# Attention and expert layer on one core: the first block's down projection, the weights' maxima and the output queue are rearranged

## The chip, the cores and the metric

The kernel runs on one core of a Trainium2 chip. The metric is the device time of one execution in microseconds (us). The inputs are float32 and lie in the chip's memory.

## The reference

The program has two parts. The first is attention: for each of 4 batches, `kv` (384 x 32 positions of 128 channels) is averaged over 4 x 4 positions, multiplied by `w_sr`, and used as keys and values of 12288 queries. The second is a layer of 8 experts over all 49152 rows x of the attention's output. Cut to what matters:

```python
a = softmax(scale * q @ k.T); x = a @ v
do = x @ w_skip > 0                      # other rows are passed on as they are
e = argmax(x[do] @ w_gate); g = softmax(x[do] @ w_gate)[e]
y = g * (relu(x @ w1[e]) @ w2[e])        # w1[e]: 128 x 1024, w2[e]: 1024 x 128
out[do] = x + y
```

## The kernel before

The attention phase takes the rows in 384 tiles of 128. When a tile group is done, its rows are written to the output and routed: the rows of each expert are scattered to a region of a scratch tensor `scr` in device memory, by GpSimd's indirect DMAs (line 192), one for 128 rows. Each row carries its gate, its row number in the output and a scale.

The expert layer then works on groups of 2048 rows of one expert, each in 4 blocks of 512 rows (`NST = 4`). Six groups of the expert that has most rows are peeled out of the loop and follow the attention in one straight program (`peel`, line 419, 24 blocks); the other groups run in a loop (line 1105) whose number of rounds is known only at run time. Here it is 12. All matrix operands are split in two float16 halves, high and low, and a product is a sum of three: high x high, high x low and low x high. In the peel and in the loop each engine runs its instructions in the order in which the program emits them.

A block s works as follows.

- `finish` (line 323) empties the accumulators of the block before: VectorE computes gate x y + x from the accumulator's first 128 columns (line 342), ScalarE takes the second 128 columns (line 330), GpSimd adds both (line 335) and scatters the rows to the output (line 192), in 4 tiles of 128 rows. The row numbers are read from column C + 1 of the block's x tile `xin`. In the peel, VectorE copies them first (line 354), since there the rows are put in a queue, `out_rows`, and scattered later.
- `up` (line 291) computes 8 chunks of h = relu(x @ w1): three products of 512 columns each (lines 296 to 298) into one of 4 PSUM buffers, from which ScalarE takes the high half (line 299) and VectorE the low half (line 300).
- `gates` (line 319) makes the block's factors on VectorE.
- `x_transpose` (line 280) splits the x of the block after next (ScalarE line 282, VectorE line 285) and transposes it by a DMA on SP's queue (line 289).
- `load_x` (line 197) loads the x of a coming block into the buffer that the block before has left.
- `down` (line 303) adds h @ w2 into 4 accumulators: for each of 8 chunks k, four products of high h with the 256 columns of w2's high and low halves, which lie side by side in `w2_hl`, and, one chunk later, four products of low h with the 128 columns of the high half (line 309).

The weights of the next group come in over the four blocks. In block 0, `split_w2` (line 274) splits this group's w2: ScalarE writes the high half (line 275), VectorE the low half (line 276), and a copy of the output scale follows (line 278). Then the next w1 and w2 are loaded (lines 257, 260). In block 1, `w_scale` (line 200) takes the largest magnitude of each (line 209) and writes them on two diagonals (line 217). In block 2 one product spreads them over the partitions (line 220) and the scales follow. In block 3, `split_w1` (line 230) splits w1.

The rows in the peel are sent by `scatter_next` (line 363), which is called five times per block, at its top, after up chunks 0, 1 and 3 and inside the down projection, and a sixth time after chunk 5 if no row for `scr` is left. It sends a row tile to `scr` if one is left and at most 20 output row tiles (`(HOLD - 1) * TT`) are queued, and an output row tile otherwise. `finish` queues two of a block's four tiles at the block's top and two after chunk 3. The buffers of the output rows are 6 (`HOLD`), taken in turn, so a block's `finish` must wait until the rows of the sixth block before are written. The loads of the loop's first weights are emitted in the step in which no row for `scr` is left (`flush`, line 920), on SP's queue.

The loop is divided into stages, one block each, and an engine enters a stage only when all have left the stage before last; `previous_stage_wait` (line 1113) puts that wait at a place of its own on an engine. On SP in block 0, the loads of the weights stand behind the first four up chunks, and the load of x stands ahead of the transpose.

Of the kernel before, what the change touches and what calls it, by code (L numbers as in the profile page):

```python
# [25 lines left out]
def kernel(  # L26
# [142 lines left out]
    h, paced, scr_rows, out_rows, first_p, held = {}, {}, [], [], [], []  # L169
# [30 lines left out]
    def w_scale(halves=False):  # L200
        em = emask.broadcast_to([P, 2])
        for i, w in enumerate((w1_raw, w2_raw.rearrange("p k c -> p (k c)"))):
# [5 lines left out]
            else:  # L208
                nc.vector.tensor_reduce(out=w_max[:, i:i + 1], in_=w, axis=AX.X, op=ALU.max, apply_absolute_value=True)
        if halves:  # L210
            nc.vector.tensor_reduce(out=w_max, in_=w_part, axis=AX.X, op=ALU.max)
# [4 lines left out]
        for i in range(2):  # L216
            eng.tensor_scalar(out=w_dg[:, i, :], in0=ident_bf, scalar1=wf[:, i:i + 1], scalar2=None, op0=ALU.mult)
# [30 lines left out]

    def load_w(gidx):
        load_expert(nc.sync.value_load(tabi[0:1, bass.ds(gidx, 1)], min_val=0, max_val=E - 1))  # L250

    def load_expert(e):
        load_w1(e)
        load_w2(e)
# [48 lines left out]
    def down(s):  # L303
        terms = []
        for c in range(FC + DL):
            terms.extend((x, k, n) for x, k, n in (("hi", c, 2), ("lo", c - DL, 1)) if 0 <= k < FC)
        for i, (x, k, n) in enumerate(terms):
            for t in range(TT):
                m = nc.tensor.matmul(ys[t][:, 0:n * C], h[x][:, k, t * P:(t + 1) * P],  # L309
                                     w2_hl[:, k, 0:n, :].rearrange("p a c -> p (a c)"), start=(i == 0),  # L310
# [12 lines left out]
    def finish(s, end=False):  # L323
        o = (first_p[0] if first_p else op).tile([P, TT, C], F32, name="o")
        o2 = None if end else op.tile([P, TT, C], F32, name="o2", bufs=1)
        ids = xin[s].bitcast(I32)
# [5 lines left out]
        def send(ts):  # L332
            for t in ts:
                if not end:
                    nc.gpsimd.tensor_tensor(out=o[:, t, :], in0=o[:, t, :], in1=o2[:, t, :], op=ALU.add)  # L335
                if first_p:
                    out_rows.append((out, kept[:, t:t + 1], o[:, t, :], NT - 1, "out"))
                else:
                    scatter_rows(out, ids[:, t, C + 1:C + 2], o[:, t, :], NT - 1, "out")

        for t in range(TT):
# [10 lines left out]
        if first_p:  # L352
            kept = first_p[0].tile([P, TT], I32, name="ids")
            nc.vector.tensor_copy(kept, ids[:, :, C + 1])
        else:
            yield
# [6 lines left out]
    def scatter_next():  # L363
        if held:
            return
        if scr_rows and len(out_rows) <= (HOLD - 1) * TT:
# [52 lines left out]
    def peel():  # L419
        LB = PEEL * NST  # L420
        for b in range(LB):
# [9 lines left out]
            for c in range(FC):  # L431
# [4 lines left out]
                if b == LB - 3 and c == 5:  # L436
                    scale = w_scale()
                if b in (LB - 3, LB - 2) and c == 5:
                    next(scale, None)
# [734 lines left out]
```

## Time and profile before

| | |
|---|---|
| median of 3 runs | 1758.96 us (1758.93 to 1760.55) |
| the profiled execution, its own time | 1756.8 us |
| its span, first to last instruction | 1754.2 us |
| TensorE busy | 1700.2 us, 97% of the span |
| VectorE, ScalarE, GpSimd busy | 87%, 75%, 66% |
| mean granted clock of TensorE | 0.997 |

The rows below and all numbers of the prediction come from the profiled execution. Times of a timeline count from the start of its span. The timeline merges neighbours of one kind: a line gives the start of the first, the time until the end of the last, and their number. Products overlap: a product of 512 columns is shown with 0.38 us, but starts 0.22 us after the one before it. So TensorE's pace is read from the starts, and its idle time in brackets, which counts from a product's shown end, is shorter than the time lost. PE is TensorE, DVE VectorE, ACT ScalarE, POOL GpSimd, SP the queue of most loads and of the transposes. The attention phase ends at about 970 us, the peel at about 1219, the loop at about 1744.

### The profile page before, as it was taken

The numbers are of one execution on the slowest core, as the hardware profiler recorded it, in microseconds if no ns is written. First come the engines' busy times: TensorE is split into PE (matmuls) and PEld (weight loads), VectorE is DVE, ScalarE is ACT, GpSimd is POOL, SyncE is SP. The second block draws the span as 40 slices with busy tenths as digits, with TensorE's granted clock in tenths as the row PEclk, the third lists the DMA queues.
The fourth block names the chain that finished last, engine by engine and source line by source line (L and its number), as shares of the span: only waits on it lengthen the run. The fifth ranks groups of instructions, "written<-read, shape, count | busy, mean of one in ns | idle before, by whom it ended". The sixth has DMA issues, their size and how long they took to land. (4 is left out here: it accounts for less than half of the span.)

```text
span 1754.2 us, 47456 instructions
## 1 busy us (share of the span) xinstructions
PE 1700.2 (97%) x16497; PEld 1393.2 (79%) x16497; DVE 1532.2 (87%) x3221; ACT 1311.9 (75%) x2683; POOL 1156.6 (66%) x1576
## 2 busy tenths in 40 slices
PE   6999999999999999999999999999999999999997
PEld 5999999999999989999998666676666666666665
DVE  7989999999999999999999867777888888888886
ACT  4888888888888888888888656666666666666664
POOL 3368778888788887666566667755555555555554
PEclk9999999999999999999999999999999999999999
DMA  7999999999899999899998663323333333333332
GB/s 237 223 240 206 194 194 245 220 198 181 173 204 199 235 210 198 184 204 189 209 204 181 176 193 115 91 78 79 98 96 97 98 97 99 101 99 97 98 96 73
DMA packets 616911, 281.07 MB, mean 160 GB/s; under 512 B 502944, under 2 KB 567072, under 8 KB 616736
## 3 DMA queue, kind: packets, MB, share of 16 engines
q1 hardware_dynamic: 590192, 231.68, 63.4%
q0 software_dynamic: 21504, 38.43, 6.7%
q10 hardware_dynamic: 5040, 8.72, 1.3%
q8 instruction: 98, 1.61, 0.4%
q14 instruction: 77, 0.63, 0.1%
HBM read 85.36 MB, written 79.72 MB: 94 GB/s over the span
## 5 line engine op out<-in xcount | busy, mean ns | idle before, releaser
L192 POOL DMA_INDIRECT scr<-rows,di x384 | 421.1, 1097 | 156.5 <-DVE nm L692 94.6
L698 ACT ACTIVATE p_sb<-s_ps,nm 128x768 f32<-128x768 f32 x384 | 346.5, 902 | 107.9 <-DVE nm L692 105.1
L692 DVE TENSOR_REDUCE nm<-s_ps 128x1 f32<-128x768 f32 x384 | 365.5, 952 | 20.7 <-PE s_ps L686 19.1
L309 PE MATMUL acc_ps<-w_hl,h_hi 128*128 128x256 f16 x2304 | 333.9, 273 | 12.2 <-DVE w_hl L276 11.2
L749 PEld LDWEIGHTS <-pt 128*128 128x128 f16 x4608 | 274.9, 97 | 63.8 <-issue 62.5
L749 PE MATMUL acc_ps<-v_hi,pt 128*128 128x138 f16 x3072 | 320.2, 224 | 2.1 <-DVE rs L757 1.6
L684 PE MATMUL s_ps<-k_hi,q_hi 128*128 128x384 f32 x768 | 293.3, 382 | 0.4 <-ACT k_hi L549 0.4
L749 PE MATMUL acc_ps<-v_lo,pt 128*128 128x138 f16 x1536 | 293.0, 223 | 0.0
L330 ACT ACTIVATE o<-acc_ps,g_sc 128x128 f32<-128x128 f32 x284 | 89.1, 369 | 271.8 <-DVE o L342 271.8
L706 DVE SCALAR_TENSOR_TENSOR p<-p_sb,p 128x512 f16<-128x512 f32 x384 | 276.0, 719 | 4.7 <-ACT p L702 3.9
L335 POOL TENSOR_TENSOR o<-o,o 128x128 f32<-128x128 f32 x284 | 141.3, 506 | 200.0 <-ACT o L330 191.8
L300 DVE SCALAR_TENSOR_TENSOR h_lo<-h_ps,h_hi 128x512 f16<-128x512 f32 x384 | 238.3, 683 | 28.1 <-ACT h_hi L299 27.6
L686 PE MATMUL s_ps<-k_hi,q_lo 128*128 128x384 f32 x768 | 259.3, 338 | 0.0
L685 PE MATMUL s_ps<-k_lo,q_hi 128*128 128x384 f32 x768 | 258.2, 336 | 1.0 <-DVE k_lo L550 1.0
L192 POOL DMA_INDIRECT out_dram<-o,xin x196 | 195.7, 998 | 83.8 <-POOL o L335 70.5
L702 ACT ACTIVATE p<-p_sb 128x512 f16<-128x512 f32 x384 | 242.2, 631 | 8.2 <-DMA pt<-p 5.3
L309 PEld LDWEIGHTS <-h_hi 128*128 128x128 f16 x2304 | 207.3, 98 | 43.3 <-issue 16.0
L299 ACT ACTIVATE h_hi<-h_ps 128x512 f16<-128x512 f32 x384 | 212.4, 606 | 5.3 <-PE h_ps L298 0.2
L309 PE MATMUL acc_ps<-w_hl,h_lo 128*128 128x128 f16 x2304 | 210.9, 219 | 0.0
L309 PEld LDWEIGHTS <-h_lo 128*128 128x128 f16 x2304 | 170.9, 98 | 11.5
L749 PE MATMUL acc_ps<-v_hi,ptq 128*128 128x138 f16 x1536 | 178.0, 223 | 0.0
L342 DVE SCALAR_TENSOR_TENSOR o<-acc_ps,g_sc,xin 128x128 f32<-128x128 f32 x288 | 81.2, 344 | 103.6 <-PE acc_ps L309 57.5
(202 smaller groups left out, 3516.0 us busy)
## 6 DMA issues: line engine op xcount, KB each, us to landing
q_sb<-in_q_dram SPq DMA_DIRECT2D x96, 256.0 KB
out_dram<-rows SPq DMA_DIRECT2D x96, 256.0 KB
xin<-scr SPq DMA_DIRECT2D x75, 264.0 KB, 2.9
kvt<-in_kv_dram SPq DMA_DIRECT2D x74, 256.0 KB
w_raw<-in_moe_w_dram SPq DMA_DIRECT2D x26, 512.0 KB, 3.7
scr<-pad ACTq DMA_DIRECT2D x32, 264.0 KB
pt<-p SPq DMA_TRANSPOSE x384
scr<-rows,di POOLq DMA_INDIRECT x384
```

Of the source, the lines that this page charges most:

```text
L192: ins = nc.gpsimd.indirect_dma_start(out=dst, out_offset=bass.IndirectOffsetOnAxis(ap=ids, axis=0), in_=src, in_offset=None, bounds_check= ...
L299: nc.scalar.activation(out=h["hi"][:, c, :], in_=ps, func=AF.Relu)
L300: paced["by"] = nc.vector.scalar_tensor_tensor(out=h["lo"][:, c, :], in0=ps, scalar=0.0, in1=h["hi"][:, c, :], op0=ALU.max, op1=ALU.subtra ...
L309: m = nc.tensor.matmul(ys[t][:, 0:n * C], h[x][:, k, t * P:(t + 1) * P], w2_hl[:, k, 0:n, :].rearrange("p a c -> p (a c)"), start=(i == 0) ...
L684: nc.tensor.matmul(s[:, h, :HK], q_hi, k_hi[:, sl], start=True, stop=False)
L685: nc.tensor.matmul(s[:, h, :HK], q_hi, k_lo[:, sl], start=False, stop=False)
L686: nc.tensor.matmul(s[:, h, :HK], q_lo, k_hi[:, sl], start=False, stop=True)
L692: paced["by"] = nc.vector.tensor_reduce(out=NM[t], in_=S_PS[t][:, :, :HK], axis=AX.XY, op=ALU.max, negate=True).ins
L698: nc.scalar.activation(out=P_SB[t], in_=S_PS.pop(t)[:, :, :HK], func=AF.Exp, bias=NM.pop(t))
L702: nc.scalar.activation(out=P16[t][:, 0, :], in_=p_flat(t)[:, 0:KD * P], func=AF.Copy, scale=2.0 ** PEXP)
L706: paced["both"] = nc.vector.scalar_tensor_tensor(out=p16[:, 1, :], in0=p_flat(t)[:, 0:KD * P], scalar=2.0 ** PEXP, in1=p16[:, 0, :], op0=A ...
L749: nc.tensor.matmul(ps[:, j % 2, :], w, v[a][:, k, :], start=(i == 0), stop=(i == len(AVL) - 1))
```

## The change

Five edits, all in the expert layer:

- `down` takes a number `apart`, which is 3 in the loop's block 0 and 0 elsewhere. With it, the products of high h with w2's high and low halves are separate (128 columns each) for the first three chunks, and the order is: hi 0, lo 0, hi 1, lo 1, hi 2 with the high half of w2, then hi 0, 1, 2 with the low half, then the rest as before. Twelve more instructions per call.
- `w_scale`: in the loop, w1's maximum is taken in block 0 and w2's in block 1; in the peel, the maxima are taken in four halves, one per block, beginning four blocks earlier. The two diagonals are made by GpSimd everywhere. In the loop w1's load moves up behind SP's wait for the stage, after the first up chunk; w2's load keeps its place.
- `scatter_next` counts two more rows (`owed`) between the top of a block and its chunk 3.
- `finish` copies the row numbers to a small tile first, in the peel on VectorE, in the loop on GpSimd, and the scatters read the copy. Of two row tiles, both additions come ahead of both scatters.
- The load of x stands behind the transpose on SP's queue.

```diff
-    def w_scale(halves=False):
+    def w_scale(halves=True):
...
             else:
                 nc.vector.tensor_reduce(out=w_max[:, i:i + 1], in_=w, axis=AX.X, op=ALU.max, apply_absolute_value=True)
+                if i == 0:
+                    yield
...
         for i in range(2):
-            eng.tensor_scalar(out=w_dg[:, i, :], in0=ident_bf, scalar1=wf[:, i:i + 1], scalar2=None, op0=ALU.mult)
+            nc.gpsimd.tensor_scalar(out=w_dg[:, i, :], in0=ident_bf, scalar1=wf[:, i:i + 1], scalar2=None, op0=ALU.mult)
...
-    def down(s):
-        terms = []
-        for c in range(FC + DL):
-            terms.extend((x, k, n) for x, k, n in (("hi", c, 2), ("lo", c - DL, 1)) if 0 <= k < FC)
-        for i, (x, k, n) in enumerate(terms):
+    def down(s, apart=0):
+        terms = [("hi", 0, 0, 1)] if apart else []
+        for c in range(1, apart):
+            terms.extend((("lo", c - 1, 0, 1), ("hi", c, 0, 1)))
+        terms.extend(("hi", c, 1, 2) for c in range(apart))
+        for c in range(apart, FC + DL):
+            terms.extend(v for v in (("hi", c, 0, 2), ("lo", c - DL, 0, 1)) if 0 <= v[1] < FC)
+        for i, (x, k, a, b) in enumerate(terms):
             for t in range(TT):
-                m = nc.tensor.matmul(ys[t][:, 0:n * C], h[x][:, k, t * P:(t + 1) * P],
-                                     w2_hl[:, k, 0:n, :].rearrange("p a c -> p (a c)"), start=(i == 0),
+                m = nc.tensor.matmul(ys[t][:, a * C:b * C], h[x][:, k, t * P:(t + 1) * P],
+                                     w2_hl[:, k, a:b, :].rearrange("p a c -> p (a c)"), start=(i == 0),
                                      stop=(i == len(terms) - 1))
...
         def send(ts):
-            for t in ts:
-                if not end:
+            if not end:
+                for t in ts:
                     nc.gpsimd.tensor_tensor(out=o[:, t, :], in0=o[:, t, :], in1=o2[:, t, :], op=ALU.add)
...
+            rows = [(out, kept[:, t:t + 1], o[:, t, :], NT - 1, "out") for t in ts]
+            if first_p:
+                out_rows.extend(rows)
+                owed[0] = TT - 1 - ts[-1]
+                return
+            for row in rows:
+                scatter_rows(*row)
+
+        ids, kept = kept, (first_p[0] if first_p else op).tile([P, TT], I32, name="ids")
+        (nc.vector if first_p else nc.gpsimd).tensor_copy(kept, ids)
...
-        if scr_rows and len(out_rows) <= (HOLD - 1) * TT:
+        if scr_rows and len(out_rows) + owed[0] <= (HOLD - 1) * TT:
...
-                if b == LB - 3 and c == 5:
+                if b == LB - 7 and c == 5:
                     scale = w_scale()
-                if b in (LB - 3, LB - 2) and c == 5:
+                if LB - 7 <= b < LB - 1 and c == 5:
                     next(scale, None)
...
                         tc.previous_stage_wait(eng.engine)
+                    if s == 0:
+                        e = expert_of(i + 1)
+                        load_w1(e)
                     next(done)
...
                     if s == 0:
-                        load_w(i + 1)
-                    load_x(load_start(i if s == 0 else i + 1), prv)
+                        load_w2(e)
                     up(s, range(XC, FC))
                     x_transpose((s + 2) % NST)
-                    if s == 1:
-                        scale = w_scale()
-                    if s in (1, 2):
+                    load_x(load_start(i if s == 0 else i + 1), prv)
+                    if s == 0:
+                        scale = w_scale(False)
+                    if s < NST - 1:
                         next(scale, None)
                     if s == NST - 1:
                         split_w1()
-                    for _ in down(s):
+                    for _ in down(s, 0 if s else 3):
                         pass
```

## Rows read from the trace of the kernel before

**Rows 1.** Waits of TensorE, 1200 to 1754: waiter, releaser, us, times, longest

```profile
PE acc_ps L309 <- DVE w_hl L276: 11.2, 11, 1.3
PE h_ps L296 <- DVE h_lo L300: 3.6, 12, 0.3
```

**Rows 2.** Timeline of TensorE, blocks of one group: start us, us, operation, idle before

```profile
1406.52 0.38 PE L296 MATMUL h_ps<-xT,w_hi 128*128 128x512 f16 x1
...
1416.98 0.38 PE L296 MATMUL h_ps<-xT,w_hi 128*128 128x512 f16 x1
...
1420.03 0.38 PE L296 MATMUL h_ps<-xT,w_hi 128*128 128x512 f16 x1 [0.30 <-DVE h_lo L300]
```

**Rows 3.** Timeline of TensorE, first block of the next group

```profile
1443.43 0.38 PE L298 MATMUL h_ps<-xT,w_lo 128*128 128x512 f16 x1
1444.78 1.03 PE L309 MATMUL acc_ps<-w_hl,h_hi 128*128 128x256 f16 x8 [0.97 <-DVE w_hl L276]
...
1449.61 0.61 PE L309 MATMUL acc_ps<-w_hl,h_lo 128*128 128x128 f16 x8
1450.06 0.38 PE L296 MATMUL h_ps<-xT,w_hi 128*128 128x512 f16 x1
```

**Rows 4.** Timeline of VectorE, end of the second block

```profile
1414.58 2.33 DVE L209 TENSOR_REDUCE w_max<-w_raw 128x1 f32<-128x1024 f32 x2
...
1417.67 1.12 DVE L342 SCALAR_TENSOR_TENSOR o<-acc_ps,g_sc,xin 128x128 f32<-128x128 f32 x4
```

**Rows 5.** Instructions of line 276: ns least, median, most

```profile
L276 DVE SCALAR_TENSOR_TENSOR w_hl<-w_raw,w_sc,w_hl x13: 1278/1285/1608, 958.1 to 1704.6; 128x1024 f16<-128x1024 f32 x13
```

**Rows 6.** Timeline of TensorE, peeled blocks

```profile
1036.33 0.38 PE L296 MATMUL up_ps<-xT,w_hi 128*128 128x512 f16 x1
...
1041.71 0.38 PE L296 MATMUL up_ps<-xT,w_hi 128*128 128x512 f16 x1 [2.62 <-DVE h_lo L300]
...
1051.26 0.38 PE L296 MATMUL up_ps<-xT,w_hi 128*128 128x512 f16 x1
```

**Rows 7.** Timeline of VectorE, peeled blocks

```profile
1039.37 1.13 DVE L342 SCALAR_TENSOR_TENSOR o<-acc_ps,g_sc,xin 128x128 f32<-128x128 f32 x4 [5.55 <-DMA out_dram<-o,ids]
```

**Rows 8.** Stretches: span, busy us by engine, granted clock, DMA share, GB/s

```profile
1042.00:1044.00 2.00, 2.00 (x8) 0.69 (x7) 2.00 (x5) 1.54 (x5) 1.39 (x3) 0.61 1.00 316
```

**Rows 9.** Timeline of VectorE, first block of a group

```profile
1443.44 1.28 DVE L276 SCALAR_TENSOR_TENSOR w_hl<-w_raw,w_sc,w_hl 128x1024 f16<-128x1024 f32 x1 [0.79 <-ACT w_hl L275]
...
1450.09 1.13 DVE L342 SCALAR_TENSOR_TENSOR o<-acc_ps,g_sc,xin 128x128 f32<-128x128 f32 x4 [1.59 <-PE acc_ps L309]
```

**Rows 10.** Page, costliest groups: busy us, mean ns, idle before

```profile
L309 PEld LDWEIGHTS <-h_lo 128*128 128x128 f16 x2304 | 170.9, 98 | 11.5
```

**Rows 11.** Timeline of SP's queue, first block of a group

```profile
1443.03 0.34 SPq L257 DMA_DIRECT2D w_raw<-in_moe_w_dram  x1
```

**Rows 12.** Loads of w_raw, 1230 to 1700

```profile
DMA to landing us min/median/max: 3.4/3.9/4.8
```

**Rows 13.** Waits of TensorE, 950 to 1220

```profile
PE up_ps L296 <- DVE h_lo L300: 3.3, 4, 2.6
```

**Rows 14.** Timeline of GpSimd, peeled blocks

```profile
1030.67 0.97 POOL L192 DMA_INDIRECT scr<-rows,di  x1 [0.30 <-DVE g_sc L320]
...
1032.70 0.99 POOL L192 DMA_INDIRECT out_dram<-o,ids  x1 [0.17 <-issue]
1034.00 0.97 POOL L192 DMA_INDIRECT out_dram<-o,ids  x1 [0.30 <-DVE x L285]
```

**Rows 15.** DMA issues: engine, count, median us to landing

```profile
out_dram<-o,xin POOLq DMA_INDIRECT x196, 2.3
```

**Rows 16.** Timeline of SP's queue, peeled blocks

```profile
1028.82 0.35 SPq L257 DMA_DIRECT2D w_raw<-in_moe_w_dram  x1
...
1033.89 1.36 SPq L289 DMA_TRANSPOSE xT<-x  x1
```

**Rows 17.** Timeline of GpSimd, second block of a group

```profile
1451.00 0.45 POOL L335 TENSOR_TENSOR o<-o,o 128x128 f32<-128x128 f32 x1 [2.93 <-ACT o L330]
```

More of the change, by code (lines that the diff above doesn't have):

```diff
@@ L168 @@
     xT = [wp.tile([P, 2 * TT, P], F16, name=f"xT{s}") for s in range(NST)]
-    h, paced, scr_rows, out_rows, first_p, held = {}, {}, [], [], [], []
+    h, paced, scr_rows, out_rows, first_p, held, owed = {}, {}, [], [], [], [], [0]
     def alloc_h(pool):
@@ L247, with expert_of @@
     alloc = {}
+    def expert_of(gidx):
+        return nc.sync.value_load(tabi[0:1, bass.ds(gidx, 1)], min_val=0, max_val=E - 1)
     def load_w(gidx):
-        load_expert(nc.sync.value_load(tabi[0:1, bass.ds(gidx, 1)], min_val=0, max_val=E - 1))
-    def load_expert(e):
+        e = expert_of(gidx)
         load_w1(e)
@@ L325, in finish @@
         o2 = None if end else op.tile([P, TT, C], F32, name="o2", bufs=1)
-        ids = xin[s].bitcast(I32)
+        kept = xin[s].bitcast(I32)[:, :, C + 1]
         def second(ts):
@@ L332, in send @@
         def send(ts):
-            for t in ts:
-                if not end:
+            if not end:
+                for t in ts:
                     nc.gpsimd.tensor_tensor(out=o[:, t, :], in0=o[:, t, :], in1=o2[:, t, :], op=ALU.add)
[L336 to L339, printed above, removed]
+            rows = [(out, kept[:, t:t + 1], o[:, t, :], NT - 1, "out") for t in ts]
[7 more added lines that the diff above has]
+        (nc.vector if first_p else nc.gpsimd).tensor_copy(kept, ids)
         for t in range(TT):
@@ L351, in finish @@
         second(early)
[L352 to L355, printed above, removed]
+        if not first_p:
             yield
@@ L901, in first_step @@
             if left in (42, 38, 34, 30, 26, 22):
-                scales.append(scales.pop() if scales else w_scale(True))
+                scales.append(scales.pop() if scales else w_scale())
                 next(scales[0], None)
```

## The prediction

> **What bounds the kernel now.** I read the waits of TensorE first, because TensorE is busy nearly all the time in the last phase, the loop over 12 groups. There almost all that it waits for has two places: the down products of each group's first block wait for the low half of w2 [rows 1], and some up products wait for VectorE's low halves of h [rows 1]. Next I read TensorE's timeline by starts, since starts give the true loss. A block without a stall takes 10.46 us, from 1406.52 to 1416.98 [rows 2]. In the first block the last up product starts at 1443.43 and the first down product at 1444.78; the down projection lasts until 1450.06, 5.28 us [rows 3], which leaves 10.46 - 5.28 = 5.18 for 24 up products, 0.216 each. So the down product could start at 1443.65. 1.13 us is lost there. In the third block the fifth chunk of up products starts at 1420.03 instead of 1416.98 + 12 x 0.216 = 1419.57 [rows 2], a loss of 0.46 us; VectorE began the evacuation 0.69 us late, at 1417.67 against 1416.98, because both maxima of the next weights, 2.33 us together, ran in the second block [rows 2, 4]. Both losses return in each group: w2's split runs 13 times, once before the loop and 12 times in it [rows 5].
>
> One more loss stands in the peeled phase ahead of the loop. The block from 1036.33 lasts until 1051.26, 14.93 us instead of 10.46, so 4.47 us are lost [rows 2, 6]. Of them 2.62 is idle time behind VectorE [rows 6]; VectorE itself waited 5.55 us, until 1039.37, for a scatter to the output that still read the buffer it was to write [rows 7]. The rest is lower clock: after the idle time the granted clock was 0.61 on the mean from 1042 to 1044, so TensorE spent most of that stretch at the lower of its two levels (1.2 and 2.4 GHz) [rows 8].
>
> **The down projection that begins narrow.** The first 20 products of the first block now need only w2's high half. VectorE begins the low half at 1443.44, released by ScalarE's high half [rows 9], so that half is there by 1443.65, and TensorE goes on without a gap. A narrow product costs 0.056 us, by the run of eight from 1449.61 to 1450.06 [rows 3]. Twenty take 1.12 us, to 1444.77. The next twelve need the low half, which released TensorE at 1444.78 [rows 3]: 0.01 us of waiting is left. A wide product costs (5.28 - 32 x 0.056) / 32 = 0.109 now, and two narrow ones 0.112, so the split of twelve costs 0.04 us. The projection ends at 1443.65 + 5.28 + 0.05 = 1448.98 instead of 1450.06: **1.08 us less per group.** The uncertain part is the low half's own length: 1285 ns mostly, but 1608 in the worst case [rows 5]. At that length 0.32 comes back per group; I take the usual length and keep 12 x 0.32 = 3.9 us for the range.
>
> The price of a narrow product in a run of 32 is not in the trace. From below it is the 0.056 of the run of eight, from above the 98 ns of a weight load [rows 10], if weight loads stop overlapping. I take 0.056, since each product in the run of eight also had weights of its own. The Trainium skill ("TensorE: Matmul & The Clock Gate", Back-to-back issue gap) gives about 81 ns for a sustained stream of load and 128-column product; by that the 32 would cost 32 x 0.025 = 0.80 us more per group, 9.6 us in all, and the time would be near 1751 us. The run of eight here does not agree with it.
>
> **The maxima spread.** w1's maximum moves to the end of the first block, w2's stays in the second, and the two small multiplications that follow go to GpSimd, where they are wanted only at the end of the third block's up products. In the first block VectorE was free at 1450.09 - 1.59 = 1448.50 [rows 9]. One maximum is 2.33 / 2 = 1.17 us [rows 4], so the evacuation that TensorE waits for could start at 1449.67. But TensorE is now done at 1448.98, so VectorE is 0.69 us late, just as late as it was before the third block. That lateness cost 0.46, and I take the same for the second block. The third block's 0.46 goes, since there VectorE, 0.69 late with both maxima, has 1.17 less to do, and begins the block only 0.69 - 0.46 = 0.23 behind TensorE. **The stall moves by one block and the sum is zero**; from below it could be gone wholly (12 x 0.46 = 5.5 us more gain), and from above it grows with the low half, which the bound above holds already.
>
> w1 must have landed by 1448.50. Its load is issued at 1443.03 now [rows 11] and not later after the change, since it is moved up on SP's queue; it takes 3.4 to 4.8 us [rows 12], so it lands by 1447.83. w2's load stays behind the low half that reads the old w2. In the peel, the halves fall on six blocks. All waits of TensorE for h's low halves from 950 to 1220 are 3.3 us, 2.6 of it the stall above [rows 13], so 0.7 is the most that spreading can give and 0 the least; I take 0.3, as one extra product in that block needs a PSUM buffer either way.
>
> **The queue that counts rows to come.** Six buffers of four rows turn around. By the rule of before, a row goes to scr when 20 or fewer are queued. In the block ahead of the one from 1036.33, at its third call, 20 are queued, so a row of scr goes out at 1030.67, ahead of the last two output rows of the oldest buffer, at 1032.70 and 1034.00 [rows 14]. Counting the two rows that are owed, the queue stands at 22 there; the output row goes first, and the fourth row moves from 1034.00 to 1032.70. With 0.99 on GpSimd [rows 14] and 2.3 to landing [rows 15], it frees the buffer at about 1035.99, before 1036.33 when it is wanted [rows 6]. The scr row takes the block's last call. It was the last one, and the loads of the loop's first weights, issued at 1028.82 as soon as no scr row is left, now come behind the block's transpose at 1033.89 [rows 16], so they no longer fill the queues while the rows are written. Next is the buffer of the block after: its last row has the same 3.6 us. **4.4 us less**; nothing if landing is as slow as it was, so 0 to 4.47.
>
> **Edits that cost nothing.** Copies of row numbers: in the peel the copy moves ahead of VectorE's evacuation into its idle time; in the loop (and behind it, for the last block) it is a new GpSimd instruction of four numbers per partition, and GpSimd idles 2.93 us ahead of a block's first addition, waiting for ScalarE [rows 17]. Uncovered, it would only delay scatters. The x load then no longer waits for scatters; behind the transpose it is passed by one DMA issue, is needed most of a block later, and the transpose gains as SP is not blocked. TensorE waits for neither now. Two additions before two scatters change only GpSimd's order.
>
> **Sum.** Loop: 12 x (1.08 + 0.46 - 0.46) = 13.0; peel 4.4 + 0.3. Together 17.7 us. The profiled execution takes 1756.8 us, which becomes 1739.1; the median of the runs is 1758.96, 2.16 higher, and becomes **1741.3**.
>
> **Rivals.** (A) The forecast, 0.62. (B) The queue cures nothing, because landing stays slow: for it, the rows are written beside pads and x loads; against it, the weight loads move away. Then 1741.3 + 4.4 = 1745.7; 0.13. (C) The change does not do what it says: the two halves interleave in one tile, and if the order kept between writer and reader is by the tile, narrow products wait for the low half as before. No row excludes that. The first block keeps its 1.13, VectorE is then in time for the second block, and the third block's stall goes: 12 x 0.46 = 5.5, with the peel's 4.7 together 10.2, so 1748.8; 0.12. (D) Narrow products run at the pace of weight loads: 32 x (0.098 - 0.056) = 1.34 per group, 16.1 in all, so 1757.4, about no change; against it the run of eight; 0.07. The rule of the Trainium skill above is a milder form of this. (E) **Slower:** VectorE waits for w1. Its maximum now sits ahead of the evacuation that TensorE needs, and VectorE works in order. If w1 lands later than 1448.50, each us of lateness costs a us per group. The gain of 17.7 is gone at 1.48 us per group, that is when the load takes 6.95 us instead of at most 4.8 [rows 11, 12]; for it speaks that an x load now goes out just ahead of it, against it that the issue is not later. At 8 us it would be 1741.3 + 12 x 2.53 = 1771.7; 0.06.
>
> **The numbers.** The range: down to 1741.3 - 5.5 - 0.4 = 1735.4 with no stall moved and all the peel's 0.7; up to 1741.3 + 4.4 + 3.9 = 1749.6 with the queue uncured and the low half at its longest. It holds B and C and leaves out D and E, 0.13: 1735 to 1750. A measurement tells 0.2%, about 3.5 us, from no change: A, B and C are faster (0.87), D is the same (0.07), E slower (0.06).
>
> **What would show it.** Right: no wait of TensorE on the first block's first down product; a run of 20 narrow products, then 12 from the low half with 0.03 to 0.35 idle; about 0.3 idle by the profile on h's low halves in the second block and none in the third; a block of 10.5 us from about 1036, clock 1.0. Wrong: a wait of about 1 us on the second half at the first narrow product (C), narrow starts clearly more than 0.056 apart (D), VectorE idle before w1's maximum on a DMA (E), VectorE's wait on the output scatter still there (B).

## The result, and the profile after

Five runs of the changed kernel have a median of 1742.36 us (1739.66 to 1744.63), five of the kernel before 1758.93 (1756.12 to 1760.55): a ratio of 0.9906, 95% interval 0.9891 to 0.992. That is 16.57 us less; the prediction was 17.7 less, 1741.3 us, and its range (1735 to 1750) holds the result.

The execution that was profiled after took 1744.63 us, with a span of 1742.3. Its span is only 11.9 us shorter than the one before, because the phase ahead of the change, whose code is the same, was longer in this execution: the first block of the peel starts at 961.80 after and at 957.17 before. In the profiles of all runs below that start lies between 957.33 and 964.70, so it scatters by itself. It enters the medians too. From there on the two are compared by TensorE's block starts:

| stretch | before, us | after, us | difference |
|---|---|---|---|
| start to first peel block | 957.17 | 961.80 | +4.63 |
| 24 peeled blocks | 263.07 | 259.93 | -3.14 |
| of them the eighth, the ninth | 14.93, 10.46 | 10.46, 11.71 | -3.22 |
| loop, first block to last | 512.50 | 499.38 | -13.12 |
| from there to the span's end | 21.5 | 21.2 | -0.3 |

Within the loop, the mean lengths of a group's four blocks (ten groups from the middle) were 11.62, 10.46, 11.02 and 10.46 us, and are 10.69, 10.76, 10.57 and 10.46. A group takes 42.48 instead of 43.57.

The waits of TensorE in the loop, which were 11.2 us behind w2's low half and 3.6 behind h's [rows 1], are these now (waiter, releaser, us in total, times, longest):

```profile
PE h_ps L299 <- PE acc_ps L315: 0.6, 1, 0.6
PE h_ps L299 <- DVE h_lo L303: 0.2, 1, 0.2
```

The view lists hardly anything, and yet two blocks of a group are longer than 10.46. So the starts are read again. TensorE's timeline of a first block and the block behind it:

```profile
1434.19 0.38 PE L299 MATMUL h_ps<-xT,w_hi 128*128 128x512 f16 x1
...
1439.16 0.38 PE L301 MATMUL h_ps<-xT,w_lo 128*128 128x512 f16 x1
1439.37 0.39 PE L315 MATMUL acc_ps<-w_hl,h_hi 128*128 128x128 f16 x4
...
1440.27 1.69 PE L315 MATMUL acc_ps<-w_hl,h_hi 128*128 128x128 f16 x20
1441.79 0.39 PE L315 MATMUL acc_ps<-w_hl,h_lo 128*128 128x128 f16 x4
...
1444.88 0.38 PE L299 MATMUL h_ps<-xT,w_hi 128*128 128x512 f16 x1
...
1447.77 0.38 PE L299 MATMUL h_ps<-xT,w_hi 128*128 128x512 f16 x1
...
1455.64 0.38 PE L299 MATMUL h_ps<-xT,w_hi 128*128 128x512 f16 x1
```

The first down product follows the last up product after 0.21 us; the gap of [rows 3] is gone. Sixteen narrow products lie between 1439.37 and 1440.27, 0.056 us each. The next sixteen and four wide ones should take 16 x 0.056 + 4 x 0.109 = 1.33, and last 1.52 until 1441.79: 0.19 is lost in there, which makes the block 10.69. In the second block the fifth chunk of up products starts at 1447.77 instead of 1444.88 + 12 x 0.216 = 1447.47: 0.30 is lost. VectorE's timeline of the same stretch says why (in brackets the idle time before, and what ended it):

```profile
1439.23 1.40 DVE L279 SCALAR_TENSOR_TENSOR w_hl<-w_raw,w_sc,w_hl 128x1024 f16<-128x1024 f32 x1 [0.85 <-ACT w_hl L278]
...
1444.31 1.21 DVE L209 TENSOR_REDUCE w_max<-w_raw 128x1 f32<-128x1024 f32 x1
1445.44 1.12 DVE L353 SCALAR_TENSOR_TENSOR o<-acc_ps,g_sc,xin 128x128 f32<-128x128 f32 x4
...
1449.43 0.74 DVE L326 TENSOR_SCALAR g_sc<-xin,y_sc 128x4 f32<-128x4 f32 x1
...
1453.53 1.20 DVE L209 TENSOR_REDUCE w_max<-w_raw 128x1 f32<-128x1024 f32 x1
...
1455.67 1.12 DVE L353 SCALAR_TENSOR_TENSOR o<-acc_ps,g_sc,xin 128x128 f32<-128x128 f32 x4 [0.47 <-PE acc_ps L315]
```

From the low half at 1439.23 VectorE has no idle time until the evacuation at 1445.44, which is 0.56 behind TensorE's block start. In the third block the evacuation waits for TensorE and not the other way round. The low half itself, 1285 ns at the median before [rows 5], has this length in the loop now (ns least, median, most):

```profile
L279 DVE SCALAR_TENSOR_TENSOR w_hl<-w_raw,w_sc,w_hl x12: 1399/1407/1431, 1226.8 to 1694.1; 128x1024 f16<-128x1024 f32 x12
```

w1's load is issued at 1438.00, well ahead of the maximum at 1444.31; the loads of w_raw land as before [rows 12]:

```profile
DMA to landing us min/median/max: 3.2/3.7/4.0
```

In the peel, the block that took 14.93 us [rows 6] is the one from 1041.11 here, and takes 10.46. The next has a stall. TensorE:

```profile
1041.11 0.38 PE L299 MATMUL up_ps<-xT,w_hi 128*128 128x512 f16 x1
...
1051.57 0.38 PE L299 MATMUL up_ps<-xT,w_hi 128*128 128x512 f16 x1
...
1054.94 0.38 PE L299 MATMUL up_ps<-xT,w_hi 128*128 128x512 f16 x1 [0.62 <-DVE h_lo L303]
...
1056.06 0.38 PE L299 MATMUL up_ps<-xT,w_hi 128*128 128x512 f16 x1 [0.31 <-issue]
...
1063.28 0.38 PE L299 MATMUL up_ps<-xT,w_hi 128*128 128x512 f16 x1
```

VectorE, whose copy of the row numbers now meets the wait of [rows 7]:

```profile
1039.94 0.17 DVE L351 COPY ids<-xin 128x4 int32<-128x4 int32 x1 [1.34 <-DMA out_dram<-o,ids]
...
1052.47 0.17 DVE L351 COPY ids<-xin 128x4 int32<-128x4 int32 x1 [3.40 <-DMA out_dram<-o,ids]
1052.60 1.13 DVE L353 SCALAR_TENSOR_TENSOR o<-acc_ps,g_sc,xin 128x128 f32<-128x128 f32 x4
```

GpSimd, the row whose landing the second of them awaits:

```profile
1047.70 0.99 POOL L192 DMA_INDIRECT out_dram<-o,ids  x1 [0.16 <-POOL o L341]
```

SP's queue, the loads of the loop's first weights, at 1028.82 before [rows 16]:

```profile
1041.06 0.36 SPq L260 DMA_DIRECT2D w_raw<-in_moe_w_dram  x1
1041.62 0.39 SPq L263 DMA_DIRECT2D w_raw<-in_moe_w_dram  x1
```

For the eighth block the buffer is free at 1039.94, 1.17 us early; its last row was issued at 1037.48, 2.46 us before. For the ninth it is free at 1052.47, 0.90 us late. Its last row was issued at 1047.70 and released VectorE 4.77 us later, where 2.3 is usual; the 2.3 of [rows 15] counts from the start of GpSimd's instruction and has its 0.99 in it. The weights' loads stand before that row. The DMA queues from 1043 to 1047 (queue, kind: packets, MB, share of the 16 DMA engines):

```profile
q1 hardware_dynamic: 1116, 0.83, 75.3%
q10 hardware_dynamic: 133, 0.25, 16.2%
q14 instruction: 1, 0.01, 0.9%
```

By the sizes and times of the packets, q1 carries SP's loads and q10 the writes of `pad` to `scr`, which ScalarE's queue issues. GpSimd issued three row tiles in this stretch, at 1043.10, 1044.39 and 1045.67, and its own queue, q0, is not in the list: not one of their packets moved while the loads did.

### The profile page after: what moved, and what is told of

Same layout as the page of the kernel before. It is cut to its first block, busy times and chain, and to the rows that moved or that the text cites. A ratio compares the mean times of both kernels' runs of the same rounds, so it can differ in the third digit from the quotient of the medians.

```text
span 1742.3 us, 47676 instructions
## 1 busy us (share of the span) xinstructions
PE 1703.1 (98%) x16641; PEld 1398.1 (80%) x16641; DVE 1525.0 (88%) x3195; ACT 1312.8 (75%) x2683; POOL 1173.2 (67%) x1654
## 5 line engine op out<-in xcount | busy, mean ns | idle before, releaser
L192 POOL DMA_INDIRECT out_dram<-o,ids x288 | 293.3, 1018 | 75.1 <-issue 44.9
L315 PE MATMUL acc_ps<-w_hl,h_hi 128*128 128x256 f16 (+1 forms) x2448 | 336.1, 266 | 0.5
L315 PEld LDWEIGHTS <-h_hi 128*128 128x128 f16 x2448 | 211.8, 98 | 29.8 <-issue 1.9
L341 POOL TENSOR_TENSOR o<-o,o 128x128 f32<-128x128 f32 x284 | 124.9, 465 | 102.8 <-ACT o L336 101.3
L757 PE MATMUL acc_ps<-v_lo,ptq 128*128 128x138 f16 x768 | 155.2, 223 | 0.0
```

Source lines behind the costliest of these rows:

```text
L192: ins = nc.gpsimd.indirect_dma_start(out=dst, out_offset=bass.IndirectOffsetOnAxis(ap=ids, axis=0), in_=src, in_offset=None, bounds_check= ...
L315: m = nc.tensor.matmul(ys[t][:, a * C:b * C], h[x][:, k, t * P:(t + 1) * P], w2_hl[:, k, a:b, :].rearrange("p a c -> p (a c)"), start=(i = ...
L757: nc.tensor.matmul(ps[:, j % 2, :], w, v[a][:, k, :], start=(i == 0), stop=(i == len(AVL) - 1))
```

## Experiments

The edits are against the changed kernel. They ran in three groups, each on one chip beside the kernel before: e1 to e4 (before 1758.37 us), e5 to e7 (before 1766.22) and e8 to e11 (before 1766.54). e1 to e8 are one execution each. On the chips of the second and third group seven or eight more peeled blocks (in e10 twelve) take 10.9 to 12.3 us, in the changed kernel too: VectorE's evacuation begins in most of them 0.8 to 0.9 us behind TensorE, mostly with no releaser in the profile. What holds it stays open. So totals are compared within a group, and otherwise the lengths of blocks, which agree to 0.02 us in the loop for the same code. This table has the means of a group's four blocks in the loop, the eighth and ninth peeled block, and the loop from its first to its last block, all in us:

| kernel | four blocks of a group | 8th, 9th | loop | time |
|---|---|---|---|---|
| before | 11.62, 10.46, 11.02, 10.46 | 14.93, 10.46 | 512.50 | 1758.93 |
| changed | 10.69, 10.76, 10.57, 10.46 | 10.46, 11.71 | 499.38 | 1742.36 |
| e1 wide first products | 11.78, 10.46, 10.57, 10.46 | 10.46, 12.01 | 508.90 | 1753.43 |
| e2 owed rows not counted | 10.69, 10.76, 10.57, 10.46 | 13.10, 10.46 | 499.55 | 1742.63 |
| e3 both maxima in block two | 10.69, 10.46, 10.57, 10.46 | 10.46, 11.83 | 495.89 | 1740.35 |
| e4 four narrow chunks | 10.50, 10.95, 10.57, 10.46 | 10.46, 11.90 | 499.39 | 1740.45 |
| e5 addition, scatter by turns | 10.57, 10.76, 10.57, 10.46 | 10.46, 11.86 | 497.83 | 1749.71 |
| e6 no row copy, early x load | 10.76, 10.76, 10.57, 10.46 | 10.46, 11.74 | 500.35 | 1749.92 |
| e7 w1's maximum in halves | 10.69, 10.46, 10.57, 10.46 | 10.46, 11.83 | 495.89 | 1745.49 |
| e8 as e3, w_dg on VectorE | 10.68, 10.46, 11.32, 10.46 | 10.46, 11.69 | 504.75 | 1756.07 |
| e9 cures together, rows first | 10.50, 10.46, 10.57, 10.46 | 10.46, 10.46 | 493.71 | 1746.63 |
| e10 cures together, more places | 10.50, 10.46, 10.57, 10.46 | 11.71, 10.46 | 493.63 | 1745.48 |
| e11 changed, again | 10.69, 10.76, 10.57, 10.46 | 10.46, 11.82 | 499.51 | 1752.31 |

The theory with which the first seven were set up: in a group's first two blocks one unbroken chain on VectorE, from w2's low half over w1's maximum to the evacuation, decides when TensorE goes on; and in the peel the queue's new count is what cures the eighth block.

**e1: the narrow start alone undone.**

```
-                    for _ in down(s, 0 if s else 3):
+                    for _ in down(s):
```

> The changed kernel with the old down projection in the loop's first block (wide products from the start); all else as changed. In the changed kernel the four blocks of a group take 10.69, 10.76, 10.57 and 10.46 us. Theory (one chain): from the high half of w2 on, VectorE runs without a gap through the low half, h's low halves, the x split and w1's maximum, and that chain alone sets when the second block may go on; narrow products only let TensorE work meanwhile. Then the first block returns to 11.59, the second falls to 10.46: 0.60 us per group, about 7 us in all. Rival (two separate stalls): the second block keeps its 0.30 and the loss is 0.90 per group, about 11 us.

The first block went to 11.78, 0.19 more than expected (0.12 of it is the low half of w2, which takes 1406 ns here, as in the changed kernel, and 1285 in the kernel before), and the second to 10.46, since TensorE is now late enough for VectorE. The loop is 9.52 us longer. The wait of [rows 1] is back in the waits of TensorE:

```profile
PE acc_ps L315 <- DVE w_hl L279: 14.0, 12, 1.3
```

So the narrow start gains 1.09 us in the first block and hands 0.30 of it to the second: 0.79 per group, 9.5 in all. The second block's return is the chain's mark; the amount lies between the chain's 7 and the rival's 11, because of the first block's 0.19 (2.2 us in twelve groups).

**e2: the queue counts only the rows that are there.**

```
-        if scr_rows and len(out_rows) + owed[0] <= (HOLD - 1) * TT:
+        if scr_rows and len(out_rows) <= (HOLD - 1) * TT:
```

> The changed kernel without counting the owed rows. Theory: the row of scr goes ahead of the output rows again and the weights' loads fall among them, so the peeled block 7 returns from 10.46 to about 14.9 us, and block 8, which takes 11.71 in the changed kernel, returns to 10.46, since the oldest rows then have a head start of one more: 3.2 us in all. Rival: block 8's 1.25 us comes from something else (the weights' loads, the moved copy) and stays; then 4.5 us.

Both missed: the stall is back in the eighth block, but as 2.64 us, and the ninth has none. The changed kernel loses 1.25 in the ninth, and 1.4 to 1.6 in e1, e3 and e4 on the chip of this run, so the count is worth 1.1 to 1.4 us. VectorE waits as long as it did before [rows 7]:

```profile
1040.01 0.17 DVE L351 COPY ids<-xin 128x4 int32<-128x4 int32 x1 [5.30 <-DMA out_dram<-o,ids]
```

and so does TensorE (2.62 before, [rows 6]):

```profile
1042.45 0.38 PE L299 MATMUL up_ps<-xT,w_hi 128*128 128x512 f16 x1 [2.48 <-DVE h_lo L303]
```

What differs is behind the wait. Before, the granted clock was 0.61 from 1042 to 1044 [rows 8]; here it is 1.00 (span, busy us of PE, PEld, DVE, ACT and POOL, clock, DMA share, GB/s):

```profile
1042.00:1044.00 2.00, 1.55 (x8) 0.72 (x8) 2.00 (x4) 2.00 (x6) 1.62 (x2) 1.00 0.99 251
```

By the starts, the wait before cost 1041.71 - 1036.33 - 2.59 = 2.79 of the 4.47 us in [rows 2, 6], and the lower clock the other 1.68, and this one did not come back with the wait. Why the clock fell behind 2.62 us of idle time and not behind 2.48 was not tried; each is one execution.

**e3: both maxima at the end of the second block, as before the change.**

```
-                if i == 0:
-                    yield
...
-                    if s == 0:
+                    if s == 1:
                         scale = w_scale(False)
-                    if s < NST - 1:
+                    if s in (1, 2):
                         next(scale, None)
```

> The changed kernel with both maxima of the loop in the second block again, the diagonals still on GpSimd. Theory: the second block's 0.30 is the price of w1's maximum in the first block, the third block's 0.46 that of both in the second; so 10.69, 10.46, about 11.0 (a little less, since the diagonals are off VectorE), 10.46: 0.1 to 0.16 us per group worse, 1 to 2 us in all. Rival: the second block's 0.30 has another cause and stays, then 0.4 per group, 5 us.

The third block's stall did not come back: the loop is 3.49 us shorter, not longer. VectorE's timeline, both maxima in one row and the evacuation behind them:

```profile
1449.99 2.34 DVE L209 TENSOR_REDUCE w_max<-w_raw 128x1 f32<-128x1024 f32 x2
...
1452.78 1.13 DVE L351 SCALAR_TENSOR_TENSOR o<-acc_ps,g_sc,xin 128x128 f32<-128x128 f32 x4
```

and TensorE's block start:

```profile
1452.57 0.38 PE L297 MATMUL h_ps<-xT,w_hi 128*128 128x512 f16 x1
```

The evacuation is 0.21 behind, where it was 0.69 [rows 2, 4], with the same two maxima ahead of it. In [rows 4] 0.76 us lay between the end of the maxima (1416.91) and the evacuation (1417.67), here 0.45 (1452.33 to 1452.78). What left that place are the two scaled identities, w_dg, which the change gave to GpSimd. The other 0.17 of the 0.48 lies ahead of the maxima, in the four splits of x, the first of which took 520 ns before and 341 in e3. Before the change (VectorE, and the addition on GpSimd beside it):

```profile
1413.35 1.31 DVE L285 SCALAR_TENSOR_TENSOR x<-xin,x 128x128 f16<-128x128 f32 x4
1413.23 0.47 POOL L335 TENSOR_TENSOR o<-o,o 128x128 f32<-128x128 f32 x1
```

and in e3, with no addition beside them:

```profile
1448.94 1.13 DVE L286 SCALAR_TENSOR_TENSOR x<-xin,x 128x128 f16<-128x128 f32 x4
```

That made a second theory, for e8: the third block is cured without the spreading, by the edit that moved w_dg; the spreading itself costs 0.30 in each second block.

**e4: four narrow chunks.** The edit is `down(s, 0 if s else 4)`.

> The changed kernel with four chunks apart instead of three. With three, the products of the low half wait about 0.2 us for it. Theory (one chain): four cover that wait, so the first block falls to about 10.51, and the second rises by the same, to about 10.94, because VectorE is no earlier; the sum of both stays at 21.45 and the time is unchanged. Rival (two separate stalls): 10.51 and 10.76, 0.18 per group, 2.2 us faster.

As the chain has it: the first block loses its 0.19, the second grows by 0.19, and the loop is the same to 0.01 us. The waits of TensorE show where it went:

```profile
PE h_ps L299 <- DVE h_lo L303: 3.6, 11, 0.3
```

**e5: GpSimd's addition and scatter by turns, as before the change.**

```
-            if not end:
+            if first_p:
...
-            for row in rows:
-                scatter_rows(*row)
+            for t, row in zip(ts, rows):
+                if not end:
+                    nc.gpsimd.tensor_tensor(out=o[:, t, :], in0=o[:, t, :], in1=o2[:, t, :], op=ALU.add)
+                scatter_rows(*row)
```

> The changed kernel with GpSimd's old order in the loop: addition, scatter, addition, scatter. In the changed kernel the low half of w2 takes 1407 ns (median) instead of 1285, and the two additions end on GpSimd just as it begins. Theory: it is the second addition, running when VectorE begins, that stretches the low half; with the old order it takes about 1285 again, VectorE's chain is 0.12 earlier, the first block about 10.56 and the second 10.76: 0.12 per group, 1.5 us faster. Rival: the order has nothing to do with it; the blocks stay within 0.02.

The low half is back at its old length:

```profile
L279 DVE SCALAR_TENSOR_TENSOR w_hl<-w_raw,w_sc,w_hl x12: 1283/1285/1286, 1233.3 to 1699.3; 128x1024 f16<-128x1024 f32 x12
```

The first block is 0.12 shorter, as much as the low half, and the loop 1.55. So GpSimd's new order made VectorE's instruction longer. The second block stays at 10.76: TensorE and VectorE are both 0.12 earlier.

**e6: no copy of the row numbers in the loop, the x load ahead of the transpose again.**

```
-            rows = [(out, kept[:, t:t + 1], o[:, t, :], NT - 1, "out") for t in ts]
+            rows = [(out, kept[:, t:t + 1] if first_p else xin[s].bitcast(I32)[:, t, C + 1:C + 2], o[:, t, :], NT - 1, "out") for t in ts]
...
+                    load_x(load_start(i if s == 0 else i + 1), prv)
                     up(s, range(XC, FC))
                     x_transpose((s + 2) % NST)
-                    load_x(load_start(i if s == 0 else i + 1), prv)
```

> The changed kernel without the copy of the row numbers in the loop (scatters read them from x again) and with the x load back ahead of the transpose, where it waits for those scatters. Theory: both were free and brought nothing, since no transpose and no x is late for TensorE in either kernel; all four blocks stay within 0.05. Rival: holding SP behind the scatters costs, because the early load of w1 now makes its queue matter; the first or second block is longer by more than 0.1.

Between the two: the first block is 0.07 longer, the others are the same. The low half again:

```profile
L279 DVE SCALAR_TENSOR_TENSOR w_hl<-w_raw,w_sc,w_hl x11: 1473/1474/1642, 1231.8 to 1657.5; 128x1024 f16<-128x1024 f32 x11
```

It is 67 ns longer, which is the block's 0.07. GpSimd's second additions begin at 1444.25 here, 0.50 ahead of the low half, where in the changed kernel the pair begins 0.57 ahead (1438.66 and 1439.23). The copies and the load order thus show no cost of their own; they shift where GpSimd's additions meet VectorE's low half. Which of the two edits does so was not tried.

**e7: w1's maximum in two halves, one at the end of the first block, one in the second.** The reduction over half of w1 is written twice, with the `yield` between, and a third joins the two results.

> The changed kernel with w1's maximum in the loop taken in two halves, one in the first block and one in the second ahead of w2's, and joined there. Theory: VectorE is late for the second block by 0.55 and TensorE bears about 0.25 of it; half a maximum is 0.6 us less, so the second block's 0.30 goes, and the third block stays at 10.57 if the second has the room (VectorE idles 0.47 there now): 0.30 per group, 3.6 us faster. Rival: the room is not there, and the third block rises by what the second gains.

As expected: second block 10.46, loop 3.49 us shorter. Half a maximum (0.6 us) less in the chain is enough.

**e8: e3, and w_dg made by VectorE again.**

```
-            nc.gpsimd.tensor_scalar(out=w_dg[:, i, :], in0=ident_bf, scalar1=wf[:, i:i + 1], scalar2=None, op0=ALU.mult)
+            eng.tensor_scalar(out=w_dg[:, i, :], in0=ident_bf, scalar1=wf[:, i:i + 1], scalar2=None, op0=ALU.mult)
```

> Beside the changed kernel: both maxima of a group are taken at the end of the second block, as in the kernel before (as in the run e3_bothmax), and in addition the loop's two scaled identities (w_dg) are made by VectorE again. New theory: the third block's wait of the kernel before (blocks of 11.03 us) went because these two instructions left VectorE's chain between the maxima and the next block's first evacuation, not because the maxima were spread. Without them that evacuation began 0.21 us after the block; with them (0.34 us longer) it begins about 0.55 us after, which in the changed kernel's second block cost 0.30: third blocks of 10.57 + 0.3 = 10.9 us, 1743 to 1745 us on a chip where the kernel before takes 1758.4. Rival: the earlier load of w1 or the order of the loads did it: third blocks stay 10.57 us.

The third block is 11.32, so its rival falls and w_dg on VectorE does cost what the second theory said, but the whole price was 0.75, not 0.3. TensorE shows two parts:

```profile
1462.95 0.38 PE L297 MATMUL h_ps<-xT,w_hi 128*128 128x512 f16 x1
...
1465.83 0.38 PE L297 MATMUL h_ps<-xT,w_hi 128*128 128x512 f16 x1
...
1468.88 0.28 PE L220 MATMUL h_ps<-w_dg,ones_bf 128*128 128x256 bf16 x1 [0.30 <-DVE h_lo L301]
```

The fifth chunk comes at 1465.83 instead of 1462.95 + 2.59 = 1465.54, the 0.29 that was expected. A second wait follows at 1468.88. VectorE:

```profile
1463.14 0.42 DVE L217 TENSOR_SCALAR w_dg<-ident_bf,w_exp 128x128 bf16<-128x128 bf16 x2
1463.47 1.12 DVE L351 SCALAR_TENSOR_TENSOR o<-acc_ps,g_sc,xin 128x128 f32<-128x128 f32 x4
...
1467.48 0.75 DVE L324 TENSOR_SCALAR g_sc<-xin,y_sc 128x4 f32<-128x4 f32 x1
```

The evacuation is 0.52 behind TensorE; and the small product for g_sc, usually 0.22, takes 0.75, since it now falls beside GpSimd's pair of additions:

```profile
1467.71 0.89 POOL L339 TENSOR_TENSOR o<-o,o 128x128 f32<-128x128 f32 x2
```

The kernel before lost 0.46 there: 0.29 goes with w_dg, as here, and the other 0.17 is as much as its long split of x (e3).

**e9, e10, e11: the cures together, and the changed kernel beside them.** e9 and e10 have four narrow chunks, both maxima in the second block, and addition and scatter by turns. For the peel, e9 writes `len(out_rows) + owed[0] <= (HOLD - 1) * TT - 2`, and e10 gives a seventh place for a scatter in every block (`if kind == "up" and c == 5:`).

> Beside the changed kernel: four chunks narrow and not three; both maxima at the end of the second block; GpSimd's addition and scatter by turns; and in the peel rows of the first writes go only where at least two rows fewer are held. Theory (each wait has its own cause, and the cures add up): blocks of a group 10.5, 10.46, 10.57, 10.46 (42.0 us in place of 42.48: 5.8 us over twelve groups), and the ninth peel block 10.46 in place of 11.71, as its buffer's last row goes out one or two places sooner: 7 us below the changed kernel's time, ratio to the kernel before about 0.987. Rival for the peel: the last first write moves behind, and with it the loads of the weights; the same wait then shows on the tenth or eleventh block, and only 5.8 us are won.

> Beside the changed kernel: the same three edits of the loop (four narrow chunks, both maxima in the second block, addition and scatter by turns), and in the peel seven places for scatters in every block from the first on, where the changed kernel gives the seventh only once the first writes are out. Theory: the loop's group 42.0 us; in the peel the last first write and the last row that the ninth block's buffer waits for both leave several places sooner, so the eighth and ninth blocks take 10.46: 7 us below the changed kernel. Rival: GpSimd is then busy past its share in the first eight blocks, its additions come late, and blocks one to six grow by some tenths each, as much as the ninth block wins.

> The changed kernel itself, beside the two before it on the same chip: groups of 42.48 us, eighth and ninth peel blocks 10.46 and 11.71 us, ratio to the kernel before 0.990 to 0.992.

Ratios to the kernel before on that chip: e9 0.9885 (0.9866 to 0.9905), e10 0.9884 (0.9869 to 0.9899), the changed kernel 0.992 (0.9907 to 0.9934). The medians of e9 and e10 are 5.7 and 6.8 us below the changed kernel's. The loop gave what was expected, 5.80 and 5.88 us; the waits of TensorE list a single one there, of 0.5 us, and 10.57 in the third block is 10.46 and the weights' small product of 0.11. One of e9's four executions took 3190 us, at a mean granted clock of 0.77; it was not the profiled one, nothing on record explains it, and ratio and median leave it out.

In the peel neither gave what was hoped. In e9 the eighth and ninth block are clean, and all 24 take 264.59 against 265.61 in e11, 1.0 less. In e10 they take 267.53, 1.9 more: as its rival had it, blocks three to eight grow, by 0.4 to 1.3 each; VectorE begins them 0.7 to 1.2 us late, about as late as the unexplained blocks of these chips, so whether GpSimd's work is the reason is not shown. The loads of the weights were issued at 1064.83 in e9, 1022.74 in e10, 1029.44 in e2, 1041.06 in the changed kernel. In e2 and the changed kernel the stall stands in the block after the loads, in e10 it grows there too (11.39, 11.71), in e9 no block right behind them has one. Its sixteenth takes 12.28 instead of e11's 11.14, which gives back 1.1 of what the ninth won; that one is among the unexplained blocks, 13 to 19 in e9 and 11 to 18 in e11.

e9's ninth block was not cured by the row's going out sooner, as expected. Its buffer's last row leaves at 1050.56, and the block starts at 1054.42: 3.86 us, where the changed kernel has 3.87 (1047.70 to 1051.57). What differs is that no weights are loaded then. While e9 issues the three rows ahead of that one (1045.95, 1047.25, 1048.53), the queues from 1045.85 to 1049.85 are these:

```profile
q10 hardware_dynamic: 435, 0.82, 56.8%
q1 hardware_dynamic: 144, 0.27, 22.2%
q0 software_dynamic: 62, 0.13, 9.5%
```

`pad` is written here too, and the rows' packets move beside it. So the loads hold up the rows, as far as the queues and the equal lead of the last row show it; no run moves the loads and nothing else.

## Why the prediction was right, point by point

- **The sum.** Predicted was 17.7 us less; the medians differ by 16.57, and loop, peel and end by 13.12 + 3.14 + 0.3 = 16.5 in the profiles. That both agree so well is partly chance, since the start of the peel scatters by 7 us. The loop's 13.0 was right to 0.1, because the errors of the first two blocks cancelled. They had to: VectorE's chain sets when the second block goes on, so what TensorE loses in the first it need not wait for in the second (e4, where 0.19 moves from one to the other).
- **The narrow start: right, 0.18 per group too large.** "Twenty take 1.12 us" and "The next twelve need the low half": so it went, and 16 narrow products took 0.056 us each. That rules out (D). The Trainium skill's 81 ns per product ("TensorE: Matmul & The Clock Gate", Back-to-back issue gap) does not agree with this stream either, which has new weights for each product. The step that was mis-sized is "I take the usual length": the low half took 1407 ns instead of 1285, and the block 10.69 instead of 10.51. That is 0.12 of the 0.18; the rest is that the products began 0.14 us after the low half, and not 0.21 as reckoned (1443.44 to 1443.65), so they came to its end sooner. The bound of 0.32 per group holds it. The cause was put at nothing: "Two additions before two scatters change only GpSimd's order". They make VectorE's low half longer (e5), which costs 1.55 us in the loop.
- **(C) the halves ordered by the tile: wrong.** The first narrow products start 0.14 us after the low half began to be written into the same tile, and wait for nothing.
- **The maxima: right in the sum, the reason not needed.** "The stall moves by one block and the sum is zero": it is 0.30 in the second block and none in the third, 0.16 less per group. The reason given, that VectorE "has 1.17 less to do" in the third block, is true of the changed kernel, where VectorE idles 0.47 there, but it is not what the cure depends on: with all 2.33 back the block is 10.57 all the same (e3). The two multiplications that left for GpSimd, which I had only in passing, are enough together with the shorter split of x: 0.31 and 0.17 of the 0.69 that VectorE was late. Whether the spreading alone would have been enough too was not run. Spreading the maxima costs 3.5 us beside the other edits, and the kernel without it is better (e3, e7).
- **The queue: the eighth block right, the ninth wrong.** "Next is the buffer of the block after: its last row has the same 3.6 us" held: it had 3.87. What failed is the landing time, put at 2.3 there too, with the loads that "no longer fill the queues while the rows are written": the same edit moves them ahead of this row, and it took 4.77 us from its issue. The sum 0.99 + 2.3 counts GpSimd's 0.99 twice; the eighth block's row took 2.46 in all. The peel gave 3.1 instead of 4.7. And the count alone is worth 1.1 to 1.4 (e2); the stall of 4.47 before had 1.68 of lower clock in it, which did not come back in e2, so that part of the gain may be luck.
- **The peel's maxima.** 0.3 was taken; by the last seven peeled blocks it was 0.08 (+0.18, -0.35, +0.09). The 0.35 is not safe: the same block takes 11.42 again in e3, e4, e8 and e9, and 11.09 in the other runs.
- **(E) VectorE waits for w1: wrong.** The load is issued 6.3 us ahead of the maximum and lands in 4.0 at most.

## What to carry to other kernels

Where a chain on one engine sets when another goes on, price each small instruction in it: two scaled identities of 0.2 us each and one drawn-out split of x made a stall of 0.46 us that two maxima of 1.2 us got the blame for. A change of several edits should be undone edit by edit, also where the sum came out: here one of them cost 3.5 us and another 1.6, and taking both back, with a fourth narrow chunk, gave 5.8 us more. And an instruction's length is not its own while another engine works beside it: after an edit of GpSimd's order, look at VectorE's durations again. Last, a load that is moved out of the way of one transfer stands in the way of another: look at which queue's packets move while a row waits.

## What was not expected of the hardware

VectorE and GpSimd hold each other up. In the kernel before, GpSimd's addition began 0.05 us after the low half [rows 9] and took 1.54 us instead of 0.47:

```profile
1443.49 1.54 POOL L335 TENSOR_TENSOR o<-o,o 128x128 f32<-128x128 f32 x1
```

In the changed kernel the pair of additions is under way when the low half starts at 1439.23; now the low half is longer, and the scatter behind, which is 0.98 elsewhere, takes 1.79:

```profile
1438.66 0.87 POOL L341 TENSOR_TENSOR o<-o,o 128x128 f32<-128x128 f32 x2
1439.70 1.79 POOL L192 DMA_INDIRECT out_dram<-o,ids  x1 [0.17 <-POOL o L341]
```

The small product for g_sc never took more than 239 ns in the loop before, and up to 1117 after (ns least, median, most; first the kernel before):

```profile
L320 DVE TENSOR_SCALAR g_sc<-xin,y_sc x43: 220/221/239, 1236.1 to 1693.3; 128x4 f32<-128x4 f32 x43
```

```profile
L326 DVE TENSOR_SCALAR g_sc<-xin,y_sc x44: 220/243/1117, 1237.0 to 1695.6; 128x4 f32<-128x4 f32 x44
```

How much longer the low half gets goes with how far GpSimd's addition reaches into it: 0.13 us in e5, and it takes its 1285 ns; 0.31 in the changed kernel, and it takes 0.12 us more; 0.38 in e6, and it takes 0.19 more. So in these runs about 0.19 of the overlap is free, and the rest is added in full. The first split of x before the change (e3) fits: 1413.23 + 0.47 - 1413.35 = 0.35 of overlap, and it takes 520 ns instead of 340.

The Trainium skill ("SBUF — State Buffer", Who interferes with whom) says that a VectorE instruction with two inputs in SBUF contends with a GpSimd instruction that reads SBUF, and that the order of issue decides which of them blocks. In the rows of the low half and of x's split (e3) the one that starts second is the longer, as it says. For g_sc the starts do not show it: in e8 it begins at 1467.48, 0.23 ahead of the additions, and still takes 0.75.
